# Top-k attention followed by a tanh-shrink FFN: the transposes of the attention weights leave the matrix engine

## Chip, cores and metric

The program runs on one core of a Trainium2 chip. The metric is the device time of one execution in microseconds (us). The kernel before took 1729.18 us, the median of three runs (1728.87 to 1730.15).

The engines, as the profile names them: PE multiplies matrices (PEld loads its weights), DVE is VectorE, ACT is ScalarE, POOL is GpSimd, and SP does nothing here but issue DMAs. Each engine takes its own instructions in the order in which they were written; across engines only semaphores hold them together.

## What is computed

```
# 8 batches, 8 heads, 576 rows, 64 columns; float64 weights w_in (512, 2048), w_out (2048, 512)
scores = scale * np.matmul(q, k.transpose(0, 1, 3, 2))
kth = np.partition(scores, -32, axis=-1)[..., -32:-32 + 1]
scores = np.where(scores >= kth, scores, -1000000000.0)
attn = np.exp(scores - np.max(scores, axis=-1, keepdims=True))
attn = attn / (np.sum(attn, axis=-1, keepdims=True) + 1e-09)
x = np.matmul(attn, v)      # then (B, H, S, D) -> (B*S, H*D) = (4608, 512)
h = x @ w_in
out = (h - np.tanh(h)) @ w_out
```

In words: of each row of 576 scores the 32 largest are kept and go through a softmax, the values are weighted with it, and the result goes through two layers with h - tanh(h) between them. The file gives w_in and w_out as 8-byte floats; the kernel makes 4-byte floats of them itself.

## The kernel before

**Steps.** Attention is cut into 144 steps, 18 for each batch. A normal step is two heads (`hp`, a pair of heads) by 128 query rows (`qt`); the row block is 2 x 576 scores on 128 partitions. The two steps with qt = 2a and 2a + 1 of one hp share a multiplication with the values. What is left of 576 rows after four blocks of 128 is 64 rows, and these make a "rem" step (`qt == J`) for two pairs of heads at once. The order of the steps is written out in `plan` (L472): for each batch first a = 0 (8 steps), then the 2 rem steps, then a = 1 (8 steps).

**One step through the engines.** `scores` (L209): PE multiplies queries and keys into a PSUM tile of which there is one buffer, ACT copies it to SBUF (L226). `search` (L229): DVE finds the 32nd largest score of each row by two tensor operations (L248, L249), a MAX8 pair (L251) and four rounds of MAX8 and MATCH_REPLACE8 (L256, L259). `mask` (L266): POOL makes the threshold (L275), ACT and POOL push what lies under it far down (L288, L291). `expo` (L300): ACT takes the exponential and its row sums (L304). `invert` and `spread` make reciprocals of the sums (DVE L325, POOL L335). `weigh` (L339): the values need the weights z with the keys on the partitions, so PE transposes z in nine blocks of 128 x 128 (L357, L363) and ACT copies the result from PSUM into `et` and `e4` (L360, L364). `values` (L368): PE multiplies these with v (L384), ACT copies (L396), and POOL scales by the reciprocals into xT (L406, or L401 for rem steps).

**FFN.** When the 8 steps of a batch and an a are done, 256 rows of x are complete (a "unit"; every four batches the rem rows make one more). `done` names the step that completes a unit. Its FFN (`ffn_h` L420, `ffn_o` L442) is put into a list of 32 pieces, and `deal` (L544) hands them out in four places of every loop turn, so many in each that the list is empty when the next unit comes.

**The loop** (L553) is a software pipeline. Turn n works on several steps at once: it transposes step n-2, masks n-1, searches n, forms the scores of n+1, takes the exponential of n-1, and multiplies the values of n-2. Loads of q and k (L165, L166) and v (L176, L177) stand at the end of some turns in the SP queue, and so do the output DMAs (L458) among the pieces of the FFN. The loads are needed in the first 8 steps of each batch.

**The start.** During the first 17 turns (`EARLY`) the FFN's weights are loaded from the ACT queue (L117 the raw words, L119 the same bytes shifted by three) and converted by DVE, ACT and POOL between the rounds of `search` (`between`, L532): one piece of 128 x 512 in each turn at first, four in turn 9, three in turns 10 to 15. Three buffers hold raw pieces; when a piece is finished, the load of the piece three later is issued.

Of the kernel before, what the change touches and what calls it, by code (L numbers as in the profile page):

```python
# [42 lines left out]
def kernel(  # L43
# [17 lines left out]
    N = 2 * P  # L61
    CD = DM // P
    CF = DFF // P
    WJ = 4
    FJ = CF // WJ
    scale = 1.0 / float(D) ** 0.5
# [12 lines left out]
    abpool = pool("ab", 2)  # L79
    mpool = pool("m", 3)  # L80
    zpool = pool("z", 2)
    etpool = pool("et", 1)
    xpool = pool("x", 2)
    xrpool = pool("xr", 1)
    thpool = pool("th", 4)
    gpool = pool("g", 4)
    rawpool = pool("raw", 3)
    shpool = pool("shifted", 3)
    sc_ps = pool("sc_ps", 1, space=PS)
    zt_ps = pool("zt_ps", 2, space=PS)  # L90
    h_ps = pool("h_ps", 2, space=PS)
# [168 lines left out]
                cur = nxt  # L260
            between(i)

    tbs = consts.tile([P, 2, B * NHP * J + 2 * B], FP32, name="tbs")
    b8s = consts.tile([P, 2, B * NHP * J + 2 * B], FP32, name="b8s")

    def mask(n, exact):  # L266

        x = st[n]
        sc, m = x["sc"], x.pop("m")
        scf = sc[:].rearrange("p t s k -> p t (s k)")  # L270
        if exact:
            nc.gpsimd.tensor_scalar(tbs[:, :, n], m[:, :, TOP - 1], BIG, None, ALU.mult)
        else:
            for t in range(2):
                nc.gpsimd.tensor_scalar(  # L275
                    tbs[:, t, n : n + 1],
                    m[:, t, TOP - 1 : TOP],
                    m[:, t, TOP - 9 : TOP - 8],
                    BIG,
                    ALU.min,  # L280
                    ALU.mult,
                )
        nb = mpool.tile([P, 2], FP32, tag="nb", name="nb")
        nc.gpsimd.tensor_scalar(nb[:], m[:, :, 0], -scale, None, ALU.mult)
        z = zpool.tile([P, 2 * S], FP32, tag="z", name="z")
        zv = z[:].rearrange("p (t k) -> p t k", t=2)
        for t in range(2):
            nc.scalar.activation(  # L288
                zv[:, t, :], scf[:, t, :], AF.Relu, bias=tbs[:, t, n : n + 1], scale=-BIG
            )  # L290
            nc.gpsimd.tensor_tensor(zv[:, t, :], scf[:, t, :], zv[:, t, :], ALU.subtract)  # L291
        if not exact:
            nc.gpsimd.tensor_scalar(
                b8s[:, :, n], x.pop("ab")[:, :, S2 + 7], BIG, None, ALU.mult
            )
        x.update(z=z, zv=zv, nb=nb)

    rds = {}
# [35 lines left out]
            rx = rxs[n] = xpool.tile([P, 2, 2, D], FP32, tag="rx", name="rx")  # L334
            nc.gpsimd.tensor_copy(rx[:, 0:nq], rd[:].unsqueeze(3).to_broadcast([P, nq, 2, D]))  # L335

    ets = {}

    def weigh(n):  # L339


        g, z = steps[n], st[n]["z"]
        if g.rem:
            o = 0
        else:
            o = (g.qt % 2) * P
        if o:
            et, e4 = ets[n - 1]
        else:
            et = etpool.tile([P, 2, J, N], FP32, tag="et", name="et")  # L350
            e4 = etpool.tile([P, N], FP32, tag="e4", name="e4")
        ets[n] = et, e4
        for t in range(2):
            zt = zt_ps.tile([P, 512], FP32, tag="zt", name="zt")
            m0 = t * (S + R)
            for c in range(J):
                nc.tensor.transpose(  # L357
                    zt[:, c * P : (c + 1) * P], z[:, m0 + c * P : m0 + (c + 1) * P], ident[:]
                )
            nc.scalar.copy(et[:, t, :, o : o + P], zt[:].rearrange("p (c j) -> p c j", c=J))  # L360
        yield
        zt = zt_ps.tile([P, 512], FP32, tag="zt", name="zt")
        nc.tensor.transpose(zt[:, 0:P], z[:, JP : JP + P], ident[:])  # L363
        nc.scalar.copy(e4[:, o : o + P], zt[:, 0:P])  # L364
        st.pop(n)
        yield

    def values(n):  # L368

        g = steps[n]  # L370
        if not g.rem and g.qt % 2 == 0:
            return
        et, e4 = ets.pop(n)
        ets.pop(n - 1, None)
        rx = rxs.pop(n)
        nq = 1 if g.rem else 2
        w = nq * P
        av = zt_ps.tile([P, 2, N], FP32, tag="zt", name="av")
        for i in range(2 if g.rem else 1):
            cols = half(i) if g.rem else slice(0, N)  # L380
            hp = g.hp + i
            for c in range(J + 1):
                for t in range(2):
                    nc.tensor.matmul(  # L384
                        av[half(t), 0, cols],
                        vb[g.b, hp][:, t, c, :] if c < J else vr[g.b, hp][:, t, :],
                        et[:, t, c, cols] if c < J else e4[:, cols],
                        start=(c == 0),
                        stop=(c == J),
                    )  # L390
        for i in range(nq):
            nc.tensor.transpose(  # L392
                av[:, 1, i * P : (i + 1) * P], rx[:, i].rearrange("p t d -> p (t d)"), ident[:]
            )
        xs = xrpool.tile([P, 2, N], FP32, tag="xs", name="xs")
        nc.scalar.copy(xs[:, :, 0:w], av[:, :, 0:w])  # L396
        if g.rem:
            u = rests[g.b // 4]
            for i in range(2):
                o = g.b % 4 * R  # L400
                nc.gpsimd.tensor_tensor(  # L401
                    xt(u)[:, g.hp + i, o : o + R], xs[:, 0, half(i)], xs[:, 1, half(i)], ALU.mult
                )
        else:
            u = units[g.b, g.qt // 2]
            nc.gpsimd.tensor_tensor(xt(u)[:, g.hp, :], xs[:, 0], xs[:, 1], ALU.mult)  # L406
        if n in done:
            work.extend(ffn(done[n]))

# [62 lines left out]
    def plan():  # L472
        units.clear(), rests.clear(), steps.clear(), first.clear(), done.clear()

        def block(b, qt):
            return [(slice(0, P), out[b * S + qt : b * S + qt + JP : J, :])]

        def rem_block(b):
            return [(half(i), out[(b + i) * S + JP : (b + i + 1) * S, :]) for i in range(2)]

        for b in range(B):
            first.append(len(steps))
            if b % 4 == 0:
                rests.append(Unit([rem_block(b), rem_block(b + 2)], "xTr"))
            for a in range(2):
                units[b, a] = Unit([block(b, 2 * a), block(b, 2 * a + 1)], "xT")
                for hp in range(NHP):
                    steps.extend([Step(b, hp, 2 * a), Step(b, hp, 2 * a + 1)])
                done[len(steps) - 1] = units[b, a]
                if a == 0:  # L490
                    steps.extend([Step(b, hp, J) for hp in range(0, NHP, 2)])
                    if b % 4 == 3:
                        done[len(steps) - 1] = rests[-1]

    def run(exact):
        plan()
# [6 lines left out]
        pairs = [(b, hp) for b in range(B) for hp in range(NHP)]  # L503
        at(-4, lambda: load_kq(*pairs[0]))
        for i, (b, hp) in enumerate(pairs):
            n = first[b] + 2 * hp
# [12 lines left out]
        for m in range(EARLY):  # L519
# [5 lines left out]
            seq += [(2, i) for i in mine[-1:]]  # L525
            for x, (part, i) in enumerate(seq):
                parts.setdefault((m, 3 * x // max(len(seq) - 1, 1)), []).append((part, i))
        for piece in pieces[:3]:
            next(piece)
        converted = [0 if pieces else 2 * WJ * FJ]  # L530

        def between(i):  # L532
            for part, k in parts.pop((n, i), []):
                next(pieces[k])
                if part == 2:
                    converted[0] = k + 1
                    if k + 3 < len(pieces):
                        next(pieces[k + 3])
            if i == 0 and 0 <= n - 2 and n < EARLY:
                invert(n - 2)  # L540

        credit, share = 0.0, [0.0]

# [6 lines left out]
                credit -= 1  # L550
            credit = min(credit, 1.0)

        for n in range(-4, NS + 2):  # L553
            here = lambda i: 0 <= n + i < NS
            more = min([m + 2 for m in done if m + 2 >= n], default=n)
            share[0] = len(work) / (more - n + 1)
            if here(-2):
                if n >= EARLY:
                    spread(n - 2)
                w = weigh(n - 2)  # L560
                next(w)
            if here(-1):
                mask(n - 1, exact)
            if here(0):
                search(n, exact, between)
            if here(-2) and n < EARLY:
                spread(n - 2)
            deal(0.4)
            if here(1):
                scores(n + 1)  # L570
            if here(-2):
                next(w)
# [5 lines left out]
            if here(-2):  # L578
                values(n - 2)
            deal(0.2)  # L580
            for fn in todo.pop(n, []):
                fn()
# [8 lines left out]

    bad = xpool.tile([P, 2, NS], FP32, tag="bad", name="bad")
    nc.vector.tensor_tensor(bad[:], b8s[:], tbs[:], ALU.is_gt)
# [39 lines left out]
```

## Time and profile before

| | before |
|---|---|
| runs | 1729.18 us median (1728.87 to 1730.15) |
| profiled execution | 1729.38 us, of which the span of the instructions is 1727.5 us |
| mean granted clock of PE | 0.967 (0.79 up to 262 us, then 1.00) |
| PE busy | 1597.1 us, 92% |
| DVE busy | 1158.4 us, 67% |
| ACT busy | 1090.0 us, 63% |
| POOL busy | 891.3 us, 52% |
| DMA | 105741 packets, 73.03 MB |

The span is the time from the first to the last instruction on the engines; the profiled execution's time is 1.9 us longer. The share of busy time alone doesn't say what sets the end, because it is an average over a start and a steady part which differ. In the trace the instruction L248 on DVE marks the start of each search; there are 144 of them. Search 17, the first after the weights are converted, starts at 261.9 us, search 143, the last, at 1634.2 us.

### The profile page before, as it was taken

What the parts mean: (1) busy time and instruction counts of PE and PEld (TensorE: products, weight loads), DVE (VectorE), ACT (ScalarE), POOL (GpSimd) and SP (SyncE); (2) the same over time, 40 slices, a digit from 0 to 9 for tenths busy, and PEclk for the clock granted to TensorE, in tenths of its full rate; (3) what the DMA queues carried; (4) which work ended last, traced back from release to release, by engine and by line L of the source; (5) the groups of instructions that cost most, each with busy time, mean ns of one, the idle gap of its engine ahead of it and who ended that gap; (6) DMA issues with size and microseconds to landing.
All of it is one profiled execution on the core that took longest, in us unless ns stands there. A gap on an engine that the chain in (4) does not pass through costs nothing.

```text
span 1727.5 us, 25418 instructions
## 1 busy us (share of the span) xinstructions
PE 1597.1 (92%) x8386; PEld 1038.7 (60%) x8386; DVE 1158.4 (67%) x3635; ACT 1090.0 (63%) x2133; POOL 891.3 (52%) x1373
## 2 busy tenths in 40 slices
PE   3545669999999999999999999999999999999998
PEld 2324446757575757575666665757575757575664
DVE  5886777678777777733767787678776877743700
ACT  4766667757675767644666577757675767643631
POOL 2555654646464655542545564647464655543620
PEclk9766789999999999999999999999999999999999
DMA  6434532100210011000020002100110011000000
GB/s 182 133 106 176 182 103 56 35 13 1 52 44 13 2 47 49 7 7 13 21 54 21 13 7 54 36 13 1 48 48 7 7 34 48 7 7 13 1 13 14
DMA packets 105741, 73.03 MB, mean 42 GB/s; under 512 B 84608, under 2 KB 92800, under 8 KB 105600
## 3 DMA queue, kind: packets, MB, share of 16 engines
q1 hardware_dynamic: 96384, 37.77, 8.5%
q10 hardware_dynamic: 9216, 33.54, 5.5%
q8 instruction: 68, 1.11, 0.3%
q14 instruction: 73, 0.60, 0.1%
HBM read 61.85 MB, written 9.44 MB: 41 GB/s over the span
## 4 chain that ended last, share of the span: by engine, by line
PE 86%; DVE 8%; ACT 4%; issue 1%; ACTq 1%; POOL 1%; DMA 0%; SPq 0%; DVEq 0%; POOLq 0%
PE ops L446 29%; PE hps L426 28%; PE av L384 9%; PE scps L218 9%; PE zt L357 7%; DVE m L256 2%; PE zt L363 2%; DVE ab L259 2%; PE av L392 2%; PE kqps L187 1%; DVE f L139 1%; ACT sc L226 1%; ACT z L288 1%; DVE f L129 0%; DVE w_out L133 0%
## 5 line engine op out<-in xcount | busy, mean ns | idle before, releaser
L291 POOL TENSOR_TENSOR z<-sc,z 128x576 f32<-128x576 f32 x288 | 401.5, 1416 | 266.5 <-ACT z L288 266.5
L446 PE MATMUL ops<-w_out,g 128*128 128x512 f32 x1152 | 527.8, 596 | 0.0
L426 PE MATMUL hps<-xT,w_in 128*128 128x256 f32 x2048 | 477.6, 384 | 0.0
L256 DVE MAX8 m<-ab 128x8 f32<-128x288 f32 (+1 forms) x1152 | 467.3, 447 | 0.0
L426 PEld LDWEIGHTS hps<-xT,w_in 128*128 128x128 f32 x2048 | 385.9, 195 | 46.4 <-issue 0.5
L259 DVE MATCH_REPLACE8 ab<-m,ab 128x288 f32<-128x288 f32 x864 | 375.4, 442 | 0.0
L446 PEld LDWEIGHTS ops<-w_out,g 128*128 128x128 f32 x1152 | 209.2, 194 | 190.1 <-issue 188.7
L440 POOL TENSOR_TENSOR g<-g,th 128x512 f32<-128x512 f32 x144 | 183.3, 1273 | 196.1 <-ACT g L439 193.2
L288 ACT ACTIVATE z<-sc,tbs 128x576 f32<-128x576 f32 x288 | 208.2, 774 | 51.4 <-POOL tbs L275 51.4
L226 ACT COPY sc<-scps 128x1152 f32<-128x1152 f32 x144 | 160.2, 1113 | 117.5 <-ACT z L288 44.9
L304 ACT ACTIVATE z<-z,nb 128x576 f32<-128x576 f32 x288 | 222.7, 779 | 15.0 <-POOL z L291 15.0
L360 ACT COPY et<-zt 128x512 f32<-128x512 f32 x288 | 157.3, 598 | 81.3 <-PE zt L357 80.6
L357 PE MATMUL zt<-ident,z 128*128 128x128 f32 x1152 | 160.5, 284 | 48.2 <-ACT z L304 37.9
L325 DVE RECIPROCAL rd<-rd 128x4 f32<-128x4 f32 x64 | 11.3, 177 | 284.7 <-POOL rd L318 284.6
L218 PE MATMUL scps<-kT,qT 64*128 64x288 f32 (+1 forms) x1280 | 187.5, 445 | 9.0 <-DVE ab L249 8.9
L357 PEld LDWEIGHTS zt<-ident,z 128*128 128x128 f32 x1152 | 139.8, 146 | 92.8 <-ACT z L304 39.9
L248 DVE TENSOR_TENSOR ab<-scps,sc 128x576 f32<-128x576 f32 x144 | 106.4, 739 | 126.7 <-ACT sc L226 98.8
L438 ACT ACTIVATE th<-hps 128x512 f32<-128x512 f32 x144 | 85.2, 592 | 132.9 <-PE hps L426 114.2
L218 PEld LDWEIGHTS scps<-kT,qT 64*128 64x128 f32 (+1 forms) x1280 | 101.2, 183 | 101.0 <-DVE m L256 31.3
L384 PE MATMUL av<-et,vb 128*64 128x256 f32 (+1 forms) x1536 | 147.8, 337 | 0.0
L384 PEld LDWEIGHTS av<-et,vb 128*64 128x64 f32 x1536 | 87.1, 140 | 61.9 <-ACT e L364 12.9
L251 DVE MAX8 ab<-ab 128x8 f32<-128x288 f32 x288 | 116.6, 446 | 0.0
(61 smaller groups left out, 1343.2 us busy)
## 6 DMA issues: line engine op xcount, KB each, us to landing
kin<-in_k_dram SPq DMA_DIRECT2D x64, 128.0 KB, 2.8
raw<-in_moe_w_in_dram ACTq DMA_DIRECT2D x16, 512.0 KB, 3.8
qin<-in_q_dram SPq DMA_DIRECT2D x64, 128.0 KB, 3.0
vb<-in_v_dram SPq DMA_DIRECT2D x64, 128.0 KB, 2.4
raw<-in_moe_w_out_dram ACTq DMA_DIRECT2D x16, 512.0 KB, 3.6
out_dram<-ot SPq DMA_DIRECT2D x32, 256.0 KB, 2.3
shifted<-in_moe_w_in_dram ACTq DMA_DIRECT2D x16, 511.5 KB, 4.8
shifted<-in_moe_w_out_dram ACTq DMA_DIRECT2D x16, 511.5 KB, 4.5
```

What stands on the lines that cost most here:

```text
L218: nc.tensor.matmul(ps[rows, t, s, 0:S2], qT[g.b, g.hp + i][half(t), qs], kT[g.b, g.hp + i][half(t), ks], start=True, stop=True,)
L226: nc.scalar.copy(sc[:], ps[:, :, :, 0:S2])
L256: nc.vector.max(m[:, t, m8], last[t] if i == rounds - 1 else cur[t])
L259: nc.vector.match_replace(nxt[t], m[:, t, m8], cur[t], NEG)
L288: nc.scalar.activation(zv[:, t, :], scf[:, t, :], AF.Relu, bias=tbs[:, t, n : n + 1], scale=-BIG)
L291: nc.gpsimd.tensor_tensor(zv[:, t, :], scf[:, t, :], zv[:, t, :], ALU.subtract)
L304: nc.scalar.activation(x["zv"][:, t, :], x["zv"][:, t, :], AF.Exp, bias=x["nb"][:, t : t + 1], scale=scale, accum_out=den[:, t : t + 1],)
L357: nc.tensor.transpose(zt[:, c * P : (c + 1) * P], z[:, m0 + c * P : m0 + (c + 1) * P], ident[:])
L384: nc.tensor.matmul(av[half(t), 0, cols], vb[g.b, hp][:, t, c, :] if c < J else vr[g.b, hp][:, t, :], et[:, t, c, cols] if c < J else e4[:, ...
L426: nc.tensor.matmul(ps[:, f % 2, :], w_in[j][:, c, fo : fo + P], u.xT[:, c, :], start=(c == 0), stop=(c == CD - 1),)
L440: nc.gpsimd.tensor_tensor(g, g, th[:], ALU.subtract)
L446: nc.tensor.matmul(cur[u][:], u.g[f // FJ][:, f % FJ, i * P : (i + 1) * P], w_out[f // FJ][:, f % FJ, :], start=(f == 0), stop=(f == CF - 1),)
```

## The change

The transposes of z leave PE. DVE turns z in 32 x 32 blocks in one instruction (`turn_z`): after it, each group of 32 partitions holds blocks that have their keys on the partitions, but the four groups hold four different groups of query rows. Sixteen DMAs within SBUF (`spread_keys`) then move each block to the partition group where its keys belong. A pair of steps shares one `zx` and one `et` buffer. The values, which read `et`, are multiplied four steps behind the scores' search rather than two. To make room in SBUF, two buffers hold raw weight pieces rather than three. The rem steps are put between the steps of a = 1 (of a = 0 in the last batch), each directly behind the two pairs of heads that it belongs to. The check at the end of whether a row needs more than was searched becomes two small POOL operations in each step in place of one.

```diff
@@ pools
+    G = 32
+    NG = P // G
+    KC = 2 * S // P
...
+    zxpool = pool("zx", 1)
     etpool = pool("et", 1)
...
-    rawpool = pool("raw", 3)
-    shpool = pool("shifted", 3)
+    rawpool = pool("raw", 2)
+    shpool = pool("shifted", 2)
@@ mask
         if not exact:
-            nc.gpsimd.tensor_scalar(
-                b8s[:, :, n], x.pop("ab")[:, :, S2 + 7], BIG, None, ALU.mult
-            )
+            ab = x.pop("ab")
+            for t in range(2):
+                nc.gpsimd.tensor_scalar(
+                    bad[:, t, n : n + 1],
+                    ab[:, t, S2 + 7 : S2 + 8],
+                    BIG,
+                    tb[:, t : t + 1],
+                    ALU.mult,
+                    ALU.is_gt,
+                )
@@ in place of weigh
+    def turn_z(n):
+        g, z = steps[n], st.pop(n)["z"]
+        i = 0 if g.rem else g.qt % 2
+        zx = zxs[n] = zxs[n - 1] if i else zxpool.tile([P, KC, NG, 2, G], FP32, tag="zx", name="zx")
+        nc.vector.transpose(
+            zx[:, :, :, i, :].rearrange("p k c j -> p (k c) j"),
+            z[:].rearrange("p (k j) -> p k j", j=G),
+        )
+    def spread_keys(n):
+        zx = zxs.pop(n)
+        zxs.pop(n - 1, None)
+        nq = 1 if steps[n].rem else 2
+        et = ets[n] = etpool.tile([P, KC, NG, 2, G], FP32, tag="et", name="et")
+        for a in range(NG):
+            for c in range(NG):
+                nc.sync.dma_start(et[group(c), :, a, 0:nq, :], zx[group(a), :, c, 0:nq, :])
@@ plan
-                done[len(steps) - 1] = units[b, a]
-                if a == 0:
-                    steps.extend([Step(b, hp, J) for hp in range(0, NHP, 2)])
+                    if hp == NHP - 1:
+                        done[len(steps) - 1] = units[b, a]
+                    if hp % 2 and a == (b < B - 1):
+                        steps.append(Step(b, hp - 1, J))
@@ run
-        for piece in pieces[:3]:
+        for piece in pieces[:2]:
...
+        def turn_at(g):
+            return 1 if g.rem else 3 - 3 * (g.qt % 2)
...
         def between(i):
             for part, k in parts.pop((n, i), []):
                 next(pieces[k])
                 if part == 2:
                     converted[0] = k + 1
-                    if k + 3 < len(pieces):
-                        next(pieces[k + 3])
+                    if k + 2 < len(pieces):
+                        next(pieces[k + 2])
             if i == 0 and 0 <= n - 2 and n < EARLY:
                 invert(n - 2)
+            if here(-2) and i == turn_at(steps[n - 2]):
+                turn_z(n - 2)
...
-        for n in range(-4, NS + 2):
+        for n in range(-4, NS + 4):
+            more = min([m + 4 for m in done if m + 4 > n], default=n)
+            if here(-4):
+                values(n - 4)
+            share[0] = len(work) / max(more - n, 1)
...
-            if here(-2):
-                if n >= EARLY:
-                    spread(n - 2)
-                w = weigh(n - 2)
-                next(w)
+            if here(-2) and n >= EARLY:
+                spread(n - 2)
             if here(-1):
                 mask(n - 1, exact)
             if here(0):
                 search(n, exact, between)
+            elif here(-2):
+                turn_z(n - 2)
+            if here(-2) and last_of_pair(n - 2):
+                spread_keys(n - 2)
...
-            if here(-2):
-                values(n - 2)
```

So in turn n the SP queue gets the sixteen DMAs of `spread_keys(n - 2)` behind the search of n, ahead of the output DMAs and loads of the same turn, and PE gets the values of step n-4 as its first work. An even step is turned after the last round of the search (i = 3), an odd one after the first (i = 0), a rem step after the second (i = 1).

More of the change, by code (lines that the diff above doesn't have):

```diff
@@ L261, in search @@
             between(i)
-    tbs = consts.tile([P, 2, B * NHP * J + 2 * B], FP32, name="tbs")
-    b8s = consts.tile([P, 2, B * NHP * J + 2 * B], FP32, name="b8s")
+    bad = consts.tile([P, 2, B * NHP * J + 2 * B], U8, name="bad")
     def mask(n, exact):
@@ L270, in mask @@
         scf = sc[:].rearrange("p t s k -> p t (s k)")
+        tb = mpool.tile([P, 2], FP32, tag="tb", name="tb")
         if exact:
-            nc.gpsimd.tensor_scalar(tbs[:, :, n], m[:, :, TOP - 1], BIG, None, ALU.mult)
+            nc.gpsimd.tensor_scalar(tb[:], m[:, :, TOP - 1], BIG, None, ALU.mult)
         else:
@@ L275, in mask @@
                 nc.gpsimd.tensor_scalar(
-                    tbs[:, t, n : n + 1],
+                    tb[:, t : t + 1],
                     m[:, t, TOP - 1 : TOP],
@@ L288, in mask @@
             nc.scalar.activation(
-                zv[:, t, :], scf[:, t, :], AF.Relu, bias=tbs[:, t, n : n + 1], scale=-BIG
+                zv[:, t, :], scf[:, t, :], AF.Relu, bias=tb[:, t : t + 1], scale=-BIG
             )
@@ L292, in mask @@
         if not exact:
-            nc.gpsimd.tensor_scalar(
-                b8s[:, :, n], x.pop("ab")[:, :, S2 + 7], BIG, None, ALU.mult
-            )
+            ab = x.pop("ab")
[4 more added lines that the diff above has]
+                    BIG,
+                    tb[:, t : t + 1],
+                    ALU.mult,
+                    ALU.is_gt,
+                )
         x.update(z=z, zv=zv, nb=nb)
@@ L335, in spread, with group @@
             nc.gpsimd.tensor_copy(rx[:, 0:nq], rd[:].unsqueeze(3).to_broadcast([P, nq, 2, D]))
[L337 to L366, printed above, removed]
+    zxs, ets = {}, {}
+    def group(a):
+        return slice(a * G, (a + 1) * G)
+    def turn_z(n):
[14 more added lines that the diff above has]
+                nc.sync.dma_start(et[group(c), :, a, 0:nq, :], zx[group(a), :, c, 0:nq, :])
     def values(n):
@@ L372, in values @@
             return
-        et, e4 = ets.pop(n)
-        ets.pop(n - 1, None)
+        et = ets.pop(n)
         rx = rxs.pop(n)
@@ L380, in values @@
             cols = half(i) if g.rem else slice(0, N)
+            es = et[:, :, 2 * i : 2 * i + 2, 0, :] if g.rem else et
             hp = g.hp + i
@@ L386, in values @@
                         vb[g.b, hp][:, t, c, :] if c < J else vr[g.b, hp][:, t, :],
-                        et[:, t, c, cols] if c < J else e4[:, cols],
+                        es[:, (J + 1) * t + c if c < J else J],
                         start=(c == 0),
@@ L392, in values @@
             nc.tensor.transpose(
-                av[:, 1, i * P : (i + 1) * P], rx[:, i].rearrange("p t d -> p (t d)"), ident[:]
+                av[:, 1, 0:w].rearrange("p (a i j) -> p i a j", a=NG, i=nq)[:, i], rx[:, i].rearrange("p t d -> p (t d)"), ident[:]
             )
@@ L405, in values @@
             u = units[g.b, g.qt // 2]
-            nc.gpsimd.tensor_tensor(xt(u)[:, g.hp, :], xs[:, 0], xs[:, 1], ALU.mult)
+            xv = xs[:].rearrange("p s (a i j) -> p s i a j", a=NG, i=nq)
+            nc.gpsimd.tensor_tensor(
+                xt(u)[:, g.hp, :].rearrange("p (i a j) -> p i a j", a=NG, i=nq),
+                xv[:, 0],
+                xv[:, 1],
+                ALU.mult,
+            )
         if n in done:
@@ L488, in plan @@
                     steps.extend([Step(b, hp, 2 * a), Step(b, hp, 2 * a + 1)])
-                done[len(steps) - 1] = units[b, a]
-                if a == 0:
-                    steps.extend([Step(b, hp, J) for hp in range(0, NHP, 2)])
-                    if b % 4 == 3:
-                        done[len(steps) - 1] = rests[-1]
+                    if hp == NHP - 1:
+                        done[len(steps) - 1] = units[b, a]
+                    if hp % 2 and a == (b < B - 1):
+                        steps.append(Step(b, hp - 1, J))
+                        if hp == NHP - 1 and b % 4 == 3:
+                            done[len(steps) - 1] = rests[-1]
     def run(exact):
@@ L505, in run @@
         for i, (b, hp) in enumerate(pairs):
-            n = first[b] + 2 * hp
+            n = next(n for n, g in enumerate(steps) if (g.b, g.hp) == (b, hp))
             turn = turn_kq(b, hp)
@@ L527, in run, with here @@
                 parts.setdefault((m, 3 * x // max(len(seq) - 1, 1)), []).append((part, i))
-        for piece in pieces[:3]:
+        for piece in pieces[:2]:
             next(piece)
         converted = [0 if pieces else 2 * WJ * FJ]
+        def turn_at(g):
+            return 1 if g.rem else 3 - 3 * (g.qt % 2)
+        def here(i):
+            return 0 <= n + i < NS
         def between(i):
@@ L551, in deal @@
             credit = min(credit, 1.0)
-        for n in range(-4, NS + 2):
-            here = lambda i: 0 <= n + i < NS
-            more = min([m + 2 for m in done if m + 2 >= n], default=n)
-            share[0] = len(work) / (more - n + 1)
-            if here(-2):
-                if n >= EARLY:
-                    spread(n - 2)
-                w = weigh(n - 2)
-                next(w)
+        for n in range(-4, NS + 4):
[5 more added lines that the diff above has]
+                spread(n - 2)
             if here(-1):
@@ L570, in run @@
                 scores(n + 1)
-            if here(-2):
-                next(w)
             if here(-1):
@@ L577, in run @@
             deal(0.2)
-            if here(-2):
-                values(n - 2)
             deal(0.2)
@@ L590 @@
         NS = run(False)
-    bad = xpool.tile([P, 2, NS], FP32, tag="bad", name="bad")
-    nc.vector.tensor_tensor(bad[:], b8s[:], tbs[:], ALU.is_gt)
     any_bad = xpool.tile([P, 1], FP32, tag="anybad", name="anybad")
```

## The prediction

> **What bounds the kernel now.** I read the busy shares first, then busy time by stretches, cut where the conversion of the weights ends and at one whole batch, then the engines' timelines in a steady stretch.
>
> ```profile
> 0.00:262.00 262.00, 144.38 (x709) 94.12 (x710) 190.06 (x514) 168.10 (x308) 134.61 (x183) 0.79 0.44 145
> 262.00:1664.50 1402.50, 1397.46 (x7486) 908.27 (x7485) 968.23 (x3122) 911.51 (x1807) 746.52 (x1182) 1.00 0.09 24
> ```
> ```profile
> 363.80:544.80 181.00, 180.43 (x1001) 117.62 (x1001) 137.00 (x442) 125.95 (x250) 102.30 (x164) 1.00 0.10 26
> ```
>
> Columns: stretch and length, then busy us (and instructions) of PE, PEld, DVE, ACT, POOL, then PE's clock, DMA share and GB/s. From 262 us on PE is never idle (1397 of 1402): the steady part is PE's. A batch of 18 steps takes 181.0, 10.06 a step, and DVE has 44 us free in it. Before 262 us PE is busy for 144; there DVE with its waits sets the pace. The chain of waits says the same:
>
> ```profile
> PE 86%; DVE 8%; ACT 4%; issue 1%; ACTq 1%; POOL 1%; DMA 0%; SPq 0%; DVEq 0%; POOLq 0%
> ```
>
> So a transpose taken off PE is worth its time in 127 of the 144 steps, if nothing else becomes late within the time saved. The next timelines show what that could be.
>
> ```profile
> 643.48 1.04 PE L357 MATMUL zt<-ident,z 128*128 128x128 f32 x8
> 644.36 1.88 PE L446 MATMUL ops<-w_out,g 128*128 128x512 f32 x4
> ...
> 647.34 0.33 PE L363 MATMUL zt<-ident,z 128*128 128x128 f32 x1
> 647.60 1.95 PE L384 MATMUL av<-et,vb 128*64 128x256 f32 x16
> ```
> ```profile
> 642.73 0.73 DVE L248 TENSOR_TENSOR ab<-scps,sc 128x576 f32<-128x576 f32 x1
> ...
> 645.49 0.07 DVE L259 MATCH_VALUE_LOAD ab<-m,ab 128x8 f32 x1
> ...
> 650.22 0.74 DVE L248 TENSOR_TENSOR ab<-scps,sc 128x576 f32<-128x576 f32 x1
> ```
>
> Read the distance from start to start: nine transposes hold PE for 0.88 + 0.26 = 1.14 us; a search without waits is 7.49, of which 2.76 lie ahead of the end of its first MAX8 round.
>
> **The change, part by part.** I count a batch (16 normal steps, that is 8 pairs, and 2 rem steps).
>
> *Removed.* 18 x 1.14 = 20.5 us of PE, which leaves 181.0 - 20.5 = 160.5, 8.9 a step. The copies L360 and L364 (157 + 39 us in all) leave ACT, which is not late; worth nothing by itself.
>
> *VectorE's turn.* No row shows it. It reads 1152 elements. From below, the 2-in-1 rate of the L129 row (0.42 us for 512) gives 0.95; from above, the L139 row (0.68 for 512 when it runs free, 0.96 mean) gives 2.16. I take the slope between the nearest rows, MAX8 (288 elements in 0.446 us) and the tensor operation L248 (576 in 0.739): 0.293 us for 288 more, so 0.739 + 2 x 0.293 = 1.33. DVE then needs 137.0 + 18 x 1.33 = 161 a batch, as much as PE. "Vector Engine (DVE) Microarchitecture Reference" of the Trainium skill, section 3.8, states one element per cycle per lane for the 32 x 32 transpose; with the 0.96 GHz of "VectorE: DVE Perf Modes", Specifications, the bare stream is 1.20 us, an estimate, and a sum by it would be some 14 us lower than mine.
>
> *The spread.* Sixteen DMAs a pair, each 32 partitions by 9 runs of 256 bytes, 72 KB, all on SP's queue. The nearest rows are the loads there:
>
> ```profile
> 662.29 0.62 SPq L166 DMA_DIRECT2D last<-in_k_dram x1
> 663.26 1.22 SPq L165 DMA_DIRECT2D qin<-in_q_dram x2
> 664.53 0.62 SPq L166 DMA_DIRECT2D last<-in_q_dram x1
> 665.20 0.59 SPq L176 DMA_DIRECT2D vb<-in_v_dram x1
> ```
>
> The start-to-start distance behind such a three-dimensional transfer is 0.63 to 0.67 us, whether it moves 32 KB or 128 KB; I take 0.64. Ends: 0.35 (output row, L458) and 0.76 (longest L165). Landing is 2.5 us after issue (median of L166; bounds 1.9, the smallest of L177, and 2.9, the median of L165). So a spread is done 15 x 0.64 + 2.5 = 12.1 us after its first issue. The DMA engines carry it: 96384 packets took 8.5% of 16 engines' span, 24 ns each, so the 19 packets that each engine gets of one transfer need 0.46, less than 0.64. "SBUF — State Buffer", section "Can I just issue two DMAs to hit both halves?", speaks against such a design: it holds that transfers on different partition ranges serialize, and the section above it gives each a fixed 2 us or so. Taken together that would be about 16 x 2.2 = 35 us a spread, an estimate, and a kernel far slower than before; the rows above disagree, since transfers issued 0.64 apart all land about 2.5 after their own issue.
>
> *The waits that come with it.* There is one zx and one et buffer. The even step of the next pair may be turned only when the spread before it has landed, and the next spread starts only when the odd step behind it has been turned. The ring is: spread 12.1, even turn 1.33, next search up to its first round 2.76, odd turn 1.33, handoffs 0.2 (an estimate: DVE started 0.03 behind POOL's rd at 642.60): 17.7 us a pair. DVE's own work for a pair is 2 x (7.49 + 1.33) + 0.18 = 17.8. So in normal pairs the ring is just hidden under DVE. Behind the waiting turn stand the next search and, through its release of the score PSUM, PE's scores.
>
> A rem step breaks this. Its turn waits for the pair's spread, its spread waits until PE has read et for the pair's values (16 + 4 matmuls L384, 2.3 us), and the next even turn waits for its spread, of sixteen DMAs too. Pair and rem together: 12.1 + 2.3 + 12.1 + 1.33 + 2.76 + 1.33 + 0.3 = 32.2 for three steps, where DVE alone needs 26.6.
>
> SP also waits in order: for a = 0 each pair issues 10 loads (6.4 us) beside 10.2 of spread, and the load L166 waits for PE's kqps transposes; the six of a load can come just ahead of a spread. I put 0.5 us a pair for that, 2 a batch (nothing to 1.8 a pair).
>
> Batch: 6 x 17.85 + 2 x 32.2 + 2 = **173.5**, 9.64 a step, against 181 before. PE gets idle time again, some 13 us.
>
> *The rest.* POOL gets two operations of 0.32 for one of 0.28: 0.36 a step, POOL stays under 70%. The values' two turns more fill the pipeline behind hidden FFN work at the end. Rem steps moved: the FFN is dealt over 9 and 9 turns rather than 10 and 8; PE's sum is the same.
>
> *The start.* A piece's load is now issued when the piece two earlier is finished. With one piece a turn it still has a turn. With three (turns 10 to 15) the third one's load is issued in the same break in which DVE wants it: DVE waits for the ACT issue and the landing (3.7 for L117, 0.4 + 4.7 for L119), about 4.5 us net of what it waits there already; 6 x 4.5, and 2 x 3.2 in turn 9, make 33. Odd turns add 7 x 1.33 = 9; even ones fall into the 2.1 us that DVE waits there for ACT's copy of the scores. Of the 42 I keep 25, since DVE's waits for ACT (51.0 for the scores, 17.8 for f up to 280 us) overlap them in part; the ends are 0 and 45. Search 17 then starts at 287 rather than 262.
>
> **The sum.** 112 steps of the remaining 121 up to step 138 go at the batch's pace: 112 x 9.64 = 1080. Nine steps, in which two units' FFNs are dealt (one unit is 128 x 0.216 + 64 x 0.43 = 55.1 on PE), are bound by PE: 160.5/2 + 55.1 = 135. From step 138 to the end: two units 110, attention 21, the last values and handoffs 4, the last unit 55.1, and 7.9 from its end to the span's: 198. 287 + 1080 + 135 + 198 = 1700, and with 1.9 around the span 1702; the profiled execution is 0.2 from the median. Forecast **1700**, 1.7% under before. By 0.2%, 3.5 us, a measurement can tell it from no change.
>
> **Rivals.**
> 1. *Fully hidden.* If a spread is cheap (0.5 us apart, towards the output row), pairs and rem steps both fit under PE and DVE: 8.95 a step, 1002 for the 112, 1624. For it: isolated issues of 0.35. Against: none of the back-to-back three-dimensional ones is under 0.54.
> 2. *SP's queue paces the kernel: slower.* The mechanism is the same ring in the same place. A batch costs 6 x (15s + 8.1) + 2 x (30s + 13) + 2 = 150s + 76.6, s the distance of two issues. At s = 0.68 it decides: there the change gives all back (179 a batch). At s = 0.75 it is 189, 10.5 a step: 1797; at 0.8, 1845. For it: the 0.67 in the rows above, waits on more semaphores at each issue.
> 3. *A slow turn.* At 2.16 us DVE needs 19.5 a pair, the rem ring 33.8: 186.6 a batch, 10.4 a step, and 6 more at the start: 1790. For it: four bytes and strided writes, no row.
> 4. *The start alone* eats more: 45 rather than 25 gives 1720.
>
> **Chances.** Forecast (1665 to 1740) 0.42: 0.33 faster, 0.04 same, 0.05 slower. Rival 1 0.18. Rival 2 0.22, rival 3 0.10. Others, rival 4 among them, 0.08: 0.02 faster, 0.01 same, 0.05 slower. Faster 0.53, same 0.05, slower 0.42. The range 1620 to 1840 takes in rival 1, rival 3 and most of 2.
>
> **What would show it.** The new DVE instruction near 1.33 us; spread DMAs 0.64 apart on SP and landing about 2.5 later; DVE idle before even turns behind a rem step (2 to 5 us) and not behind others; PE's idle time up to some 7% in the steady part with its releaser among the spread's DMAs or DVE; a batch of 173; DVE idle before the third L129 of turns 10 to 15; search 17 at 287. It is wrong if the issue distance is above 0.68 or below 0.6, if the turn costs over 1.8, or if batches show waits on other engines.

## The result and the profile after

| | before | after |
|---|---|---|
| runs | 1729.03 us median (1728.6 to 1730.15) | 1813.75 us median (1810.5 to 1816.38) |
| ratio | | 1.0488, interval 1.0469 to 1.0507 |
| span of the profiled execution | 1727.5 us | 1814.1 us |
| search 17 starts at | 261.9 us | 304.6 us |
| batches in the steady part | 181 us | 185 to 190 us |
| DMA share of q1, the queue of SP's transfers | 8.5% of 16 engines | 35.2% of 16 engines |

The kernel became 4.9% slower, where 1.7% faster was forecast. Busy time by stretches, cut at search 17, and one batch (searches 44 to 62), with the columns of the lines shown of before:

```profile
0.00:304.60 304.60, 120.63 (x528) 75.85 (x529) 214.03 (x528) 151.92 (x261) 139.58 (x194) 0.66 0.54 150
304.60:1735.00 1430.40, 1310.82 (x6318) 809.92 (x6317) 1130.14 (x3251) 762.79 (x1421) 790.96 (x1312) 0.97 0.40 77
```
```profile
588.70:774.70 186.00, 168.26 (x839) 103.40 (x839) 159.52 (x461) 105.05 (x196) 108.42 (x183) 0.98 0.43 83
```

PE, never idle before, now has 120 us of idle time in the steady part, and 18 us in a batch of 186. DVE has 26 us in the same batch. So neither engine sets the pace. The chain of waits names what does:

```profile
PE 31%; SPq 28%; DVE 18%; DMA 10%; issue 5%; ACT 3%; POOL 2%; ACTq 1%; DVEq 0%; POOLq 0%
```

SP's queue, 0% before, holds 28%, and DMA 10%. The new instruction and the waits say the same; the columns of the second fence are total, times, and the longest, in us:

```profile
L358 DVE STREAM_TRANSPOSE zx<-z 128x1152 f32<-128x1152 f32 x144 | 197.5, 1371 | 151.2 <-DMA et<-zx 130.8
```
```profile
DVE zx L358 <- DMA et<-zx: 130.8, 50, 8.6
PE av L390 <- DMA et<-zx: 87.5, 43, 6.4
PE kqps L191 <- DMA kin<-in_k_dram: 48.4, 12, 8.6
```

The turn costs what was forecast (1.37 us by its record, 1.30 from start to start, against 1.33). DVE waits 131 us ahead of it for the spread before, PE 88 us for spreads, and 48 us for loads of k (8.9 before), which now share SP's queue with the spreads.

**The ring in the trace.** A ring is a loop of waits: each link releases the next, and the last releases the first. SP's timeline of the changed kernel, one normal pair, and DVE's in the same stretch (start, length, then the idle time before the instruction and its releaser):

```profile
604.15 10.45 SPq L372 DMA_DIRECT2D et<-zx  x16
615.83 0.35 SPq L471 DMA_DIRECT2D out_dram<-ot  x1
623.03 10.55 SPq L372 DMA_DIRECT2D et<-zx  x16
```
```profile
614.62 0.83 DVE L260 MAX8 m<-ab 128x8 f32<-128x296 f32 x2
616.64 1.38 DVE L358 STREAM_TRANSPOSE zx<-z 128x1152 f32<-128x1152 f32 x1 [1.19 <-DMA et<-zx]
617.94 0.13 DVE L336 RECIPROCAL rd<-rd 128x4 f32<-128x4 f32 x1
618.00 0.72 DVE L252 TENSOR_TENSOR ab<-scps,sc 128x576 f32<-128x576 f32 x1
...
621.24 0.44 DVE L263 MATCH_REPLACE8 ab<-m,ab 128x288 f32<-128x288 f32 x1
621.59 1.37 DVE L358 STREAM_TRANSPOSE zx<-z 128x1152 f32<-128x1152 f32 x1
```

Follow it round: first issue 604.15, even turn 616.64 (12.49 later, of which DVE stood 1.19), search 618.00, odd turn 621.59, next first issue 623.03. That is 12.49 + 1.36 + 3.59 + 1.44 = 18.88 us a pair. (Of the 12.49, the last of the sixteen transfers landed 12.07 after the first issue, and the turn began 0.42 later.) So DVE waits ahead of even turns in normal pairs too, where the prediction expected no wait. The odd turn lies behind the MATCH_REPLACE8 pair of the first round, not behind the MAX8 pair.

### The profile page after: what moved, and what is told of

Its sections match the earlier page's. It is cut to its first block, busy times and chain, and to the rows that moved or that the text cites. A ratio compares the mean times of both kernels' runs of the same rounds, so it can differ in the third digit from the quotient of the medians.

```text
span 1814.1 us, 24868 instructions
## 1 busy us (share of the span) xinstructions
PE 1502.8 (83%) x7090; PEld 929.2 (51%) x7090; DVE 1344.3 (74%) x3778; ACT 925.8 (51%) x1701; POOL 942.4 (52%) x1517
## 3 DMA queue, kind: packets, MB, share of 16 engines
q1 hardware_dynamic: 485504, 122.79, 35.2%
## 4 chain that ended last, share of the span: by engine, by line
PE 31%; SPq 28%; DVE 18%; DMA 10%; issue 5%; ACT 3%; POOL 2%; ACTq 1%; DVEq 0%; POOLq 0%
SPq L372 28%; PE ops L459 11%; PE hps L439 11%; DVE zx L358 5%; DMA et<-zx 5%; PE av L390 5%; DVE m L260 3%; DVE ab L263 3%; PE scps L222 3%; DMA kin<-in_k_dram 2%; DVE ab L255 2%; DVE ab L252 2%; DVE ab L253 2%; DMA shifted<-in_moe_w_in_dram 2%; DMA shifted<-in_moe_w_out_dram 1%
## 5 line engine op out<-in xcount | busy, mean ns | idle before, releaser
L459 PE MATMUL ops<-w_out,g 128*128 128x512 f32 x1152 | 542.9, 616 | 0.0
L439 PE MATMUL hps<-xT,w_in 128*128 128x256 f32 x2048 | 489.1, 393 | 45.0 <-ACT g L452 32.1
L459 PEld LDWEIGHTS ops<-w_out,g 128*128 128x128 f32 x1152 | 215.1, 196 | 244.9 <-issue 236.3
L358 DVE STREAM_TRANSPOSE zx<-z 128x1152 f32<-128x1152 f32 x144 | 197.5, 1371 | 151.2 <-DMA et<-zx 130.8
L292 ACT ACTIVATE z<-sc,tb 128x576 f32<-128x576 f32 x288 | 207.6, 768 | 176.5 <-POOL tb L279 170.9
L390 PE MATMUL av<-et,vb 128*64 128x256 f32 (+1 forms) x1536 | 160.3, 355 | 101.9 <-DMA et<-zx 87.5
L390 PEld LDWEIGHTS av<-et,vb 128*64 128x64 f32 x1536 | 99.2, 148 | 182.6 <-issue 102.2
L414 POOL TENSOR_TENSOR xT<-xs 128x256 f32<-128x256 f32 x64 | 48.1, 752 | 277.4 <-ACT xs L402 224.4
L252 DVE TENSOR_TENSOR ab<-scps,sc 128x576 f32<-128x576 f32 x144 | 105.9, 736 | 104.7 <-ACT sc L230 73.2
L402 ACT COPY xs<-av 128x512 f32<-128x512 f32 (+1 forms) x80 | 43.5, 543 | 253.3 <-PE av L398 253.2
L253 DVE TENSOR_TENSOR ab<-scps,sc 128x576 f32<-128x576 f32 x144 | 107.4, 746 | 0.0
```

The lines of the kernel that those rows point to most:

```text
L292: nc.scalar.activation(zv[:, t, :], scf[:, t, :], AF.Relu, bias=tb[:, t : t + 1], scale=-BIG)
L358: nc.vector.transpose(zx[:, :, :, i, :].rearrange("p k c j -> p (k c) j"), z[:].rearrange("p (k j) -> p k j", j=G),)
L390: nc.tensor.matmul(av[half(t), 0, cols], vb[g.b, hp][:, t, c, :] if c < J else vr[g.b, hp][:, t, :], es[:, (J + 1) * t + c if c < J else J ...
L439: nc.tensor.matmul(ps[:, f % 2, :], w_in[j][:, c, fo : fo + P], u.xT[:, c, :], start=(c == 0), stop=(c == CD - 1),)
L459: nc.tensor.matmul(cur[u][:], u.g[f // FJ][:, f % FJ, i * P : (i + 1) * P], w_out[f // FJ][:, f % FJ, :], start=(f == 0), stop=(f == CF - 1),)
```

## The experiments

My theory: this ring (spread, even turn, piece of search, odd turn) and its worse form around a rem step set the steady part, and the two raw buffers the start. Rivals: DVE is too full with its turns; SP or the DMAs have too many bytes; the start is most of it.

### Odd turn ahead of the search

```diff
-            return 1 if g.rem else 3 - 3 * (g.qt % 2)
+            return 1 if g.rem else 3 - 4 * (g.qt % 2)
...
             if here(0):
+                if here(-2) and turn_at(steps[n - 2]) < 0:
+                    turn_z(n - 2)
                 search(n, exact, between)
```

> The odd steps are turned ahead of the search instead of behind its first round; nothing else differs from the changed kernel (1813.75 us). Ring theory: a normal pair is paced by spread 15 x 0.655 + landing 2.5 + even turn 1.3 + 3.6 of the next search + odd turn 1.3, which is 18.9 us; without the 3.6 the ring is 15.3 and VectorE's own work of 17.8 paces the pair, so steps 24 to 33 go from 18.8 to about 17.8 a pair, a batch from 188 to some 178, the kernel to 1720 to 1755. Rival, VectorE itself is too full with the turns: its work is the same, so 1805 to 1820. Rival, the queue of SP is too full: its issues are the same, so 1805 to 1820.

1742.36 us, 1.0083 of before (1.0067 to 1.0100), as expected, and 71 us under the changed kernel with the same instructions. A normal pair takes 17.6, which is DVE's own work, 2 x (7.49 + 1.30). The searches beside rem steps still take 15 to 19. The piece of search inside the ring was the cost, and a DVE or an SP that is too full would not have gained from the order.

### One spread for the two rem steps

```diff
-                    if hp % 2 and a == (b < B - 1):
-                        steps.append(Step(b, hp - 1, J))
+                    if hp == NHP - 1 and a == (b < B - 1):
+                        steps.extend([Step(b, h, J) for h in range(0, NHP, 2)])
...
-                nc.sync.dma_start(et[group(c), :, a, 0:nq, :], zx[group(a), :, c, 0:nq, :])
+                nc.sync.dma_start(et[group(c), :, a, :, :], zx[group(a), :, c, :, :])
...
-            at(n - 1, lambda b=b, hp=hp: load_v(b, hp))
+            at(n + 3, lambda b=b, hp=hp: load_v(b, hp))
```

The rem steps stand side by side, fill the two halves of one `zx`, and are handled as a pair; v is loaded four turns later. So this run moves the rem steps and the loads of v as well as saving a spread; it doesn't separate the three.

> The two rem steps of a batch stand side by side, are turned into the two halves of one zx, and share one spread (as the steps of a pair do); the loads of v are issued four turns later so that their buffers are free. 64 + 8 spreads rather than 64 + 16. Ring theory: the third spread in three steps goes away, nine pairs of 18.9 make a batch of 170 to 175 rather than 188, and the kernel takes 1690 to 1730. Rival, VectorE itself: the turns are the same 144, so no change, 1805 to 1820. Rival, the normal pairs alone carry the loss: 1790 to 1810 (only the sixteen issues fewer a batch).

1736.20 us, 1.0044 (1.0030 to 1.0059). It is 78 us under the changed kernel, though 6 over what I expected: search 17 starts 14 us later (318.6). A batch:

```profile
411.60:586.00 174.40, 168.40 (x836) 102.69 (x835) 159.81 (x462) 105.59 (x195) 108.67 (x182) 0.98 0.46 90
```

The stalls of the rem steps are gone: from search 24 to 72 none takes over 11.0 us. Nine pairs in 174.4 are 19.4 each: the ring is left, as the run with both edits shows below (167.1). It is not all, since 19.4 is 0.5 over the ring's 18.88: in this batch DVE waits only 3.7 us for spreads, and PE with its weight loads waits 13 us for v, whose loads now stand behind spreads.

### The start by itself, and the turn by itself, on the kernel before

```diff
-    rawpool = pool("raw", 3)
-    shpool = pool("shifted", 3)
+    rawpool = pool("raw", 2)
+    shpool = pool("shifted", 2)
```

with the loads issued two pieces ahead. The second run of this pair adds DVE's turn of every z into a tile that nobody reads:

```diff
+            if 0 <= n - 2 and i == 3 - 3 * (steps[n - 2].qt % 2):
+                turn_z(n - 2)
```

> The kernel before with two buffers for raw and shifted pieces rather than three, loads issued two pieces ahead; nothing else of the change. If the shorter lead of the weights' loads is what makes the start late (search 17 at 304.6 rather than 261.9 us), search 17 starts 15 to 35 us later and so does the end: 1743 to 1765. Rival, the start is late from the spreads and turns: under 5 us, 1729 to 1734.

> The kernel before with two raw buffers as in before_two_raw, and VectorE also turns z of each step into a scratch tile that nothing reads; PE still makes its transposes and no DMA is added. Ring theory: the turn costs nothing where PE sets the pace, since VectorE has 44 us a batch free and 24 go to it: the batch stays within 2 of 181, and only the odd turns of the start, some 10 us, are added to before_two_raw. Rival, VectorE itself is too full with the turns: the batch goes over 185 and the kernel is over 40 us behind before_two_raw.

Two buffers: 1756.60 us, 1.0160 (1.0143 to 1.0177); search 17 at 289.8, 27.9 later than before, and the whole as much. DVE's waits up to there name the cause: raw loads, for which the same view of the kernel before has no row, now cost 28 us (total, times, longest).

```profile
DVE f L129 <- DMA raw<-in_moe_w_out_dram: 19.0, 5, 4.0
...
DVE f L129 <- DMA raw<-in_moe_w_in_dram: 8.7, 3, 3.9
```

With the turns: 1759.93 us, 1.0181 (1.0164 to 1.0198), only 3.3 more. DVE is 159.7 us busy in a batch and the batch takes 181.0 as before, because PE decides:

```profile
370.00:551.00 181.00, 180.43 (x1001) 117.61 (x1000) 159.74 (x460) 125.98 (x251) 102.45 (x165) 1.00 0.10 26
```

The rival "DVE is too full" falls: the turns fit in.

### Issues or bytes

```diff
-                nc.sync.dma_start(et[group(c), :, a, 0:nq, :], zx[group(a), :, c, 0:nq, :])
+                for k in (slice(0, KC // 2), slice(KC // 2, KC)):
+                    nc.sync.dma_start(et[group(c), k, a, 0:nq, :], zx[group(a), k, c, 0:nq, :])
```

> The changed kernel with each of the 16 spread transfers cut into two of half the size, the same bytes. Issue theory: the ring is set by the issues on SP, 0.655 us each, so each of the 74 spreads behind the start takes 10.5 us longer and the kernel some 700 to 790 us, to 2500 to 2600. If the bytes set it (2.36 MB a pair over the 16 DMA engines, or a write rate of SBUF), the time stays within 1800 to 1840.

2565.23 us (one run). A spread is now, in SP's timeline,

```profile
798.06 20.61 SPq L373 DMA_DIRECT2D et<-zx  x32
```

32 issues in 20.61 us, 0.645 each, where 16 with the same bytes took 10.45. A batch takes 288 to 291 us instead of 185 to 190: ten spreads of 10.2 more. The number of issues sets a spread's length, not the bytes.

### Both edits of the ring

> The changed kernel with both earlier edits at once: the odd turn ahead of the search, and the two rem steps of a batch side by side with one spread. Ring theory: with the odd turn ahead of the search the ring of a pair is 10.45 of issues, 2.5 of landing and the even turn, and it ends before DVE has done its two searches and two turns, so nine pairs of a batch take 17.6 to 17.9 each, 159 to 163 us, against 174 with the rem pair alone; over 6.2 batches that takes 70 to 90 us off 1736: 1645 to 1670, with a start as late as search 17 at 307 to 322. Rival, TensorE is the next bound: PE was busy 168 us in a batch of the changed kernel, so the batch stops at 168 to 170 and the time at 1695 to 1715. Rival, the two edits buy the same waits: no better than the better of the two, 1730 to 1740.

1693.80 us, 0.9797 (0.9781 to 0.9814): faster than before, but my number was missed. The rival, PE as the next bound, came closest: its 1695 to 1715, with batches of 168 to 170, begin just above what was measured. A batch of 167.1:

```profile
409.80:576.90 167.10, 165.86 (x839) 101.66 (x838) 159.17 (x462) 105.82 (x196) 108.97 (x184) 1.00 0.47 93
```

PE is busy in 165.9 of it: PE is the bound again. It fits this that the two edits, worth 71 and 78 us by themselves, are together worth 120 and not 149. DVE's wait ahead of its turns is 18.0 us in the whole run, 17.9 of it for ACT's exponential and not for a spread, and DVE goes from one search through both turns into the next:

```profile
L359 DVE STREAM_TRANSPOSE zx<-z 128x1152 f32<-128x1152 f32 x144 | 194.2, 1355 | 18.0 <-ACT z L316 17.9
```
```profile
566.80 1.36 DVE L359 STREAM_TRANSPOSE zx<-z 128x1152 f32<-128x1152 f32 x1
568.08 0.14 DVE L337 RECIPROCAL rd<-rd 128x4 f32<-128x4 f32 x1
568.13 1.35 DVE L359 STREAM_TRANSPOSE zx<-z 128x1152 f32<-128x1152 f32 x1
569.40 0.72 DVE L253 TENSOR_TENSOR ab<-scps,sc 128x576 f32<-128x576 f32 x1
```

### Another order in the start, and evener FFN work

```diff
-        many = {9: 4} | {n: 1 for n in range(9)} | {n: 3 for n in range(10, 17)}
+        many = {15: 1, 16: 1} | {n: 2 for n in range(15)}
...
                 if part == 2:
                     converted[0] = k + 1
-                    if k + 2 < len(pieces):
-                        next(pieces[k + 2])
+                if k + 2 < len(pieces):
+                    next(pieces[k + 2])
```

In `convert` the shifted load now comes first and the raw load after one more `yield`, both on SP's queue. So the shifted load of piece k + 2 is issued behind part 1 of piece k, the raw load behind part 2.

> The run odd_pair with another order in the start: two weight pieces a step in steps 0 to 14 and one in 15 and 16 (was one a step in 0 to 8, four in 9, three in 10 to 16), a part in each of the four places of a search, the shifted load for the piece after next issued behind part one and the raw load behind part two, both on SP's queue instead of ACT's. If the two buffers cost the start only because a load is wanted in the same search in which its buffer comes free, search 17 comes 25 to 45 us earlier than in odd_pair, and the whole is 25 to 45 us shorter. Rival, the loads now stand behind the spreads in SP's queue, and take as long there: search 17 within 10 us of odd_pair's.

1630.0 us, 0.9412 (0.9384 to 0.9441): 64 less than the run before, more than the 25 to 45 expected. Search 17 starts at 255.3 instead of 318.2. In the start, DVE's waits for raw loads fell from 27.5 to 7.8 us and those for ACT's copy of the scores from 34.7 to 16.7, together 38 of the 63 us. The edit changes the pieces in a step, the queue and the order of the loads at once, and no run separates these.

The evener dealing takes only main units into account:

```diff
-            more = min([m + 4 for m in done if m + 4 > n], default=n)
+            more = min([m + 4 for m in done if m + 4 > n and done[m].tag == "xT"], default=n)
```

> The run odd_pair_start, with the FFN work shared out over the turns up to the end of the next main unit, so that the end of the rem unit one turn later doesn't press a whole main unit into one turn. In the changed kernel that turn left DVE idle 50 us around 903 to 930, but the PE work of the double section doesn't change: if PE bounds that section, 0 to 5 us; if DVE's idleness is lost time there, 15 to 40 us shorter than odd_pair_start.

1626.05 us (1625.5 to 1631.25), 0.9415 (0.9399 to 0.9432). Against 1630.0 (1620.71 to 1631.06) that is no difference, as expected if PE bounds that section. Searches 74 to 85 even take 153 rather than 145 us. DVE's idleness there is not lost time.

This version beats both kernels. Its steady part and a batch:

```profile
252.80:1560.00 1307.20, 1285.50 (x6393) 797.01 (x6394) 1126.46 (x3250) 766.89 (x1423) 792.80 (x1314) 1.00 0.43 85
341.60:508.40 166.80, 165.44 (x839) 102.36 (x838) 159.15 (x461) 105.96 (x196) 109.09 (x184) 1.00 0.47 92
```

### The same start for the two kernels compared

> The kernel before, with its turns on TensorE and its three buffers, and the start of odd_pair_start (two pieces a step, loads on SP) and the even dealing of odd_pair_start_even. It shows how much of 1626 is the new start and not the new turning. If the start is worth as much here as the two-buffer kernels lost in it, and no more: search 17 at 245 to 258 against 261.9, behind it TensorE's 181 a batch as before, 1705 to 1728. Rival, the order of the start is the gain and the turning buys nothing: 1630 to 1660.

1704.26 us, 0.9861 (0.9843 to 0.9878); search 17 at 235.8, batches 181 to 184. With three buffers the new start brings search 17 forward by 26 us, more than I expected (245 to 258), and the whole by 24.5. So the fair comparison of the two ways to turn is 1626 against 1704: turning on DVE, with its ring mended, is worth 78 us, by the ratios 0.9415/0.9861 = 0.955. The turned version reaches search 17 17 us later (252.8 against 235.8) and gains some 94 behind it.

> The changed kernel with the same new start and even dealing, and its ring as it is (odd turn inside the search, two rem spreads a batch). If the ring costs what odd_pair against the changed kernel shows (120 us), and start and ring add up: search 17 at 250 to 262, batches of 186 to 190 as in the changed kernel, 1735 to 1765. If most of the loss was the start: under 1700.

1774.11 us, 1.0261 (1.0243 to 1.0280); search 17 at 259.8, batches 185 to 189, much as in the changed kernel. Search 17 comes 45 us earlier than there, and the kernel is 40 shorter. My range ended at 1765. The start can't explain the loss: without the ring's mending the kernel stays slower than before.

## Why the prediction was wrong

The sum went from 1700 to 1814, by its own terms:

| term | forecast | measured | what it adds |
|---|---|---|---|
| DVE's turn, start to start | 1.33 | 1.30 | |
| spread, first issue to last landing | 12.1 | 12.1 | |
| handoffs in the ring | 0.2 | 0.6 | |
| search up to the odd turn | 2.76 | 3.59 | |
| normal pair | 17.85 (DVE; ring 17.7) | 18.88 (ring) | |
| pair and rem step | 32.2 | 34.1 and 38.7 (start of search 49 to start of 52, 54 to 57) | |
| batch | 173.5 | 185 to 190 (186.0 in the one shown) | |
| 112 steps | 9.64 each, 1080 | 10.51 each, 1178 | +98 |
| search 17 | 287 | 304.6 | +18 |
| nine steps with two units | 135 | 137.4 (searches 74 to 83) | +2 |
| step 138 to the end | 198 | 194.5 | -4 |

**The step that failed** is "in normal pairs the ring is just hidden under DVE". It was hidden by 0.1 us (17.72 against 17.82), by a count that put 2.76 us of search ahead of the odd turn. The code puts the turn in `between(0)`, which stands behind the MATCH_REPLACE8 pair too: 3.59, or 0.83 us more. With 0.4 more for the handoffs, most of it between the last landing and the even turn, the ring came out 1.0 above DVE's work (18.88 against 17.85). The spread itself was forecast to the tenth, with some luck: its issues lay 0.655 us apart rather than 0.64, and its transfers landed 2.2 us after issue rather than 2.5, which cancels. Of the batch shown, 186.0 = 6 x 18.88 + 34.1 + 38.7, the six normal pairs add 6.2 and the two rem places 8.4, against which 2 us had been set for SP.

**The second rem place**, 6.5 us over the forecast, is late for a reason that I had not priced: my 0.5 us a pair was for loads just ahead of a spread, and here the loads of k and q come behind two spreads:

```profile
657.42 29.01 SPq L372 DMA_DIRECT2D et<-zx  x32
686.48 1.28 SPq L169 DMA_DIRECT2D kin<-in_k_dram  x2
...
692.89 0.50 SPq L181 DMA_DIRECT2D vr<-in_v_dram  x1
696.54 11.69 SPq L372 DMA_DIRECT2D et<-zx  x16
```

The first load is issued 29 us after the first transfer ahead of it; 8 of these SP stood between the two spreads, waiting for the next odd turn. PE and DVE in the same stretch:

```profile
690.20 0.63 PE L191 MATMUL kqps<-ident,kin 128*128 128x128 f32 x4 [4.32 <-DMA kin<-in_k_dram]
...
693.69 2.37 PE L390 MATMUL av<-et,vb 128*64 128x256 f32 x16
```
```profile
703.85 0.17 DVE L336 RECIPROCAL rdr<-rdr 128x2 f32<-128x2 f32 x1 [5.31 <-POOL rdr L329]
```

PE waits for the load (48.4 us for such loads in the run). Behind it in PE's order stand the values of the pair before; only when these have read `et` does the next spread start, at 696.54. ACT's copy of these values starts at 696.90, POOL's scaling at 697.57, and behind it in POOL's order the mask of the rem step at 698.64; DVE waits for what comes of it until 703.85. In rem_pair, with one spread for both rem steps, no search stalls there.

**Rival 2** named the right ring in the right place, with the wrong trigger: it was to decide when issues lie over 0.68 us apart. They lie 0.655 apart, as forecast. The ring decided anyhow, through its DVE part. With 0.655 and the search counted right in pairs and rem places, the rival's sum gives 6 x 18.76 + 2 x 33.5 + 2 = 181.5 a batch; most of what is missing to 186.0 is the second rem place. Its sensitivity was right as well: cutting each transfer in two made each spread 10.2 us longer.

**Rivals 1 and 3** fall: issues are not 0.5 apart, and the turn is not 2.16 us. **Rival 4** had the start right, which adds 42.7 us, close to its 45, but that is only 18 of the 114 us by which the sum missed. In the runs with these alone, the two buffers are 27.9 of it (33 in the sum) and the turns 2.1 (9 in the sum). The other 12.7 come with the rest of the change, the spreads and the new order of steps; no run separates them. That the 42 of the sum, before I cut it to 25, lies so close to the measured 42.7 is luck.

**What PE gains** was too high as well. I took 20.5 us off a batch. In the mended kernels, where PE is the bound, a batch falls from 181.1 to 166.8, by 14.3. By the distances from each matmul's start to the next in one batch of either trace, the transposes of z held PE for 19.1 us rather than 20.5 (1.06 a step; the step that I had read took 1.14), and without them the FFN's matmuls take 4.1 us more and those with the values 1.5. The profile shows hardly any idle time between them; why they are slower no run shows. With 166.8 a batch, 9.27 a step, the 112 steps need 1038 us even when the ring is free, not the 1002 of rival 1.

On the price of the spread I had weighed "SBUF — State Buffer" of the Trainium skill, "Can I just issue two DMAs to hit both halves?", against the loads in the trace. The runs side with the loads: sixteen transfers between different partition groups are issued in 10.45 us and have landed 12.1 us after the first issue, each about 2.2 us after its own (KB each, then median us from issue to landing):

```profile
et<-zx SPq DMA_DIRECT2D x1024, 72.0 KB, 2.2
et<-zx SPq DMA_DIRECT2D x256, 36.0 KB, 2.0
```

One at a time, each from issue to landing, they would need 16 x 2.2 = 35. So they overlap in this time. What the section itself measured is bandwidth (two concurrent transfers moved 6% more than one), and that these transfers, 0.655 us apart, don't test.

## What to carry to other kernels

When a buffer is used once and refilled by several engines in turn, write its ring out instruction by instruction, from the code's own order, and put a margin on it: a ring that is "just hidden" by under 1% is not hidden, and moving one instruction ahead of another (here the odd turn ahead of the search) can be worth 70 us. A queue that holds transfers which wait also holds every load behind them, so load early or put transfers that wait last. When work leaves the engine that is the bound, compare the versions with the same start: here some 25 of the 102 us between before and the best version belong to the start.

## What the runs showed of the hardware

The spread's transfers, of three dimensions, were issued on SP about 0.65 us apart whatever their size: 72 KB, 36 KB and, in the run with halves, 32 to 40 KB, each landing 1.9 to 2.2 us after its issue (medians). DVE turned 1152 four-byte elements per partition in 32 x 32 blocks in 1.30 us, start to start, between the prediction's 1.33 and its estimate of the bare stream, 1.20. PE's granted clock was lower where PE had idle time: 1.00 in batches that PE bounds, 0.98 in those with gaps, 0.66 in the start of the changed kernel against 0.79 before. It did not follow the share of busy time alone: with PE busy in 46% of the start, it was 0.73 in the run with the new start and 0.80 in the one with even dealing. The same 839 matmuls were 168.3 us busy at 0.98 and 165.9 at 1.00.
